# A gated linear attention followed by top-1 experts: heads kept on their own partitions, rows turned on VectorE, experts taken in order of their counts

## The chip, the cores and the metric

One Trainium2 chip, one core of it. The metric is the device time of one execution in microseconds (us), as the median of several runs. A profiled execution gives the trace from which the durations here are read.

## What is computed

The reference has two blocks. The first is a recurrence with a complex gate per head and feature. The state is a 48 x 48 matrix per head, and 4 batches of 8 heads run over 768 steps:

```python
for t in range(S):
    new_re = ar * S_re - ai * S_im          # ar, ai: the gate, its magnitude cut at 0.999
    new_im = ar * S_im + ai * S_re
    S_re, S_im = new_re + kv, new_im        # kv = outer product of k[t] and v[t]
    y[:, :, t] = einsum('bhd,bhde->bhe', q[:, :, t], S_re)
```

The second takes the 3072 rows of 384 numbers (8 heads side by side) and sends each to the one of 8 experts with the largest logit:

```python
logits = x @ w_gate; expert_idx = argmax(logits, axis=1); gate_w = softmax(logits)[expert_idx]
out[mask] = gate_w[mask, None] * (maximum(x[mask] @ w1[e], 0.0) @ w2[e])   # w1: 384 x 1024, w2: 1024 x 384
```

With the reference's inputs the experts 0 to 7 get 354, 406, 392, 388, 370, 421, 338 and 403 rows. All numbers are float32.

## The kernel before

**Attention.** The recurrence is turned into products over chunks of 128 steps. A gate's logarithm and angle are summed along time, and with them q and k are scaled by a cosine and by a sine factor; the scaled q and k of a head are then one operand of 96 rows (48 features of part 0, the cosine, and 48 of part 1, the sine). A chunk's rows of y are the masked products of its own q and k with v, plus q times the state left by the chunks before.

The *front* (function `front`) makes the scaled q and k in ten units of 128, 256 or 384 steps, with the features of 8 heads on 128 partitions in three groups: heads 0 to 2 on partitions 0 to 47, heads 3 to 5 on 48 to 95, heads 6 and 7 on what is left. ScalarE takes logarithms, exponentials, arctangents and sines, VectorE (and GpSimd for two multiplications per unit, from unit 3 on: `EARLY`) the rest. The last two operations of a unit on VectorE are the products with the cosine (into `hz`, part 0) and with the sine (into `Z`, part 1). Then nine transfers per unit on the SP queue (L334) move rows within SBUF, so that in `hz` every head has its part 0 on partitions 0 to 47 and its part 1 on 48 to 95.

A *chunk* (function `chunk`) is done on TensorE, for all 8 heads at once:
- *turned keys* (L361): eight turnings of a head's k into `kt`, in two groups of four; not in the last chunk of a batch;
- *scores* (L368): eight products k by q, 96 rows deep, four into each of two banks of PSUM; VectorE masks each bank (`am`);
- *old state* (L380): eight products of the state `sb` with q, from the second chunk of a batch on. The outputs have 48 partitions, of even heads at 0, of odd heads at 64, so neighbours lie on two column halves of the array;
- *values* (L387): eight products of v with `am`, in two groups of four (heads 0 to 3, 4 to 7), added to the same bank as the old state. Even and odd heads alternate in each group;
- *new state* (L395): eight products of the turned keys with v, into bank 5, copied to `sb`; not in the last chunk;
- *turning products* (L403): four, which bring y into rows of tokens and make the logits beside them.

A `route` after some chunks (the last three after chunks 3, 5 and 6 of the last batch) finds each row's expert and place on VectorE, and GpSimd sends the rows with gate and token number to `xs_hbm` (L464), where each expert has 448 places.

The order of all these operations on all engines is the list `ORDER`, in base 36; a class `Plan` with costs and dependences lies behind it. Every engine runs its part of the list strictly in order, and a DMA issue on SP waits in its place too.

**Experts.** After the last route some checks set a flag (`again`) for a slow general version behind a branch, which these inputs don't take. For each expert in turn, SP loads both weights (1536 KB each, three buffers each) and its 448 rows (L575, L578). TensorE turns the rows in twelve pieces (L586), which ScalarE and VectorE copy to `xrt`. The *first layer* (L597) is 8 x 3 products of 448 columns, cut at zero into `ht` by ScalarE (L603) and VectorE (L600). The *second layer* (L611) is 3 x 8 products of 384 columns for the first 384 rows. The 64 rows left over of two neighbouring experts share one group (L626), 64 columns of the array each. VectorE scales the outputs (L566), and GpSimd scatters them (L555). The order comes from `Plan.order`, a list scheduler on costs and dependences.

Of the kernel before, what the change touches and what calls it, by code (L numbers as in the profile page):

```python
# [22 lines left out]
G = 3  # L23

BLOCKS = ((0, 48, 0, 3, 0, 0), (48, 96, 0, 3, 3, 0), (96, 128, 0, 2, 6, 0), (96, 112, 2, 3, 6, 32), (112, 128, 2, 3, 7, 32))
TU = 384
NB = 3
EARLY = 3
# [6 lines left out]
MINC = 256  # L35
# [12 lines left out]
0 2 1l 3 4 5 1n 3n 1o 1p 6 7 8 1q 1r 9 1s a b d 3p 1t 3q c 1u f 1 e 14 3r g 1v 1w j 3o 1m 24 3s 1y 1x  # L48
l m 3t k h 4r n o p 27 i q r s 3u 26 1z 20 t u 25 21 28 3v 23 22 29 v 10 3w 2a 46 6n z 2b 11 15 2c 3x 3y
17 2d 40 y 2e 12 w 7r 2f 6p 3z 6q 6r 16 13 x 18 2g 99 42 2j 41 48 43 19 47 49 44 1d 1a 2i 6s 6t 2k 6u 2l 2m 4b 2n 45  # L50
6v 4a 9b 1b 2r 2o 4c 1c 2h 9c 2s 6w 9d 1e 6x 6y 4d 4e 2v 6o 4f 4g 76 4i 4j 1f 4h 78 9e 1i 9s 6z 2t cb 1g 38 2p 70 2w 9f
4m 9g 72 71 9h 2u 1h 3c 77 3a 79 75 2x 4n 73 2q 7a 39 2z 2y 74 4l 7b 9i cd 30 31 7c ce 3d 4u 9j 4q 32 7d 4k 4p 7e 36 3e
1k cf 3g 9u 3b 4o 37 4v 7f 3f 1j 9t 3h 4y 5b 9a 7g 4w 3i 7h 3j 4s 4t 33 4x 4z 35 5c cg 50 54 9m 51 7i 5f ch 34 55 ci 59
9k 7k 9l 7l 52 5a 53 3k 5g 7j 5q 9n 5d eu cj 5s 9o 5e 3m 7q 5h 9v 7p 7n 5r 7o ck 5l 5j 9r 3l 5t 9w 7z 56 ew 5i 7m cl co
9p 9q 9x 5m 80 cc ex cn 7x 7v 5k 81 9y 82 58 5u 5w cu 9z cm 5v 57 8h 7w 8f 5x 5n a0 5o 7y cw 86 ev a1 5p 8b ey 5y cq 8i
ad cv a2 df a4 8d cp a6 a3 87 8g 8c 8e 8y 83 ez cx a7 84 8w a5 85 5z 60 f0 8n ct f1 8j 8z 8s cy 88 aa 61 8l 62 8o 8u 8x
8t 8k a9 cr 68 94 ab f2 8m ac 90 a8 hu ak 69 89 8v 6a cs 91 f3 ag cz ai 8a d0 f4 fd 8p al hv ae 92 f7 d1 b1 d2 d3 ah f6
95 af 8r ax 6b av d4 93 aj 8q hw am az d5 d6 an hx f5 ay ao aq fg d7 d9 fe db f8 96 ap bc b2 da 98 aw ar 6e f9 97 6c 63
fa de 64 d8 b3 bd b4 kw b5 hy 65 b0 hz dd 6d as be i0 fc 66 i1 ff b6 dc au fb dg fh b7 b8 67 di bf 6h 6k dh i2 fi dm 6j
# [77 lines left out]
def gateloop_then_moe(ctx, tc, gates, qk, gates_u, qk_u, v, wg, w1, w2, out):  # L137
# [11 lines left out]
    def tt(o, a, b, op, eng=None):  # L149
        (eng or nc.vector).tensor_tensor(out=o, in0=a, in1=b, op=op)  # L150
# [47 lines left out]
    with ExitStack() as att:  # L198
# [25 lines left out]
        def dve2(n):  # L224
            return n * 0.00104 + 0.06
# [18 lines left out]
        def front(u):  # L244
# [66 lines left out]
            for part in (0, 1):  # L311
                for p0, p1, g0, g1, h0, d0 in BLOCKS:
                    if part == 0 and p0 == 0:
                        continue
# [481 lines left out]
```

## Time and profile before

| | us |
|---|---|
| median of 3 runs | 570.27 |
| lowest, highest | 564.31, 571.41 |
| the profiled execution | 565.04 |
| its span, first to last instruction | 563.2 |

The profile is of one execution. A page gives busy times and the span in 40 slices. Answers of the trace give busy times by stretch, groups by line, waits, and the order of time, in which neighbouring instructions of one line are merged into one row. A float32 product shows as two records on TensorE (PE), a turning as one. [...]

### The profile page before, as it was taken

Reading aid. Unit: us, or ns where it says so; the run is one execution under the profiler, and the core shown is the slowest. Engines: PE = TensorE matmul, PEld = TensorE weight load, DVE = VectorE, ACT = ScalarE, POOL = GpSimd, SP = SyncE. Lnnn points to the kernel's source line nnn. Section 1 sums busy time; section 2 is a strip of 40 time slices with the busy share of each in tenths; the row PEclk is TensorE's granted clock in tenths of the full one; section 3 lists DMA queues with packets and bytes.
Section 4 is the critical chain, followed back from the end, with each engine's and each line's share of the span. In section 5 each row is a group of like instructions: output and inputs, shape, how many; then the busy total and the mean of one; then the engine's idle time right before and its main releaser. Section 6 shows DMA issues by size and latency. Waiting matters only on the chain. (4 is left out here: it accounts for less than half of the span.)

```text
span 563.2 us, 7082 instructions
## 1 busy us (share of the span) xinstructions
PE 485.5 (86%) x2785; PEld 329.1 (58%) x2785; DVE 240.8 (43%) x412; ACT 214.0 (38%) x313; POOL 94.3 (17%) x106
## 2 busy tenths in 40 slices
PE   0045998798898799729999999999999999999995
PEld 0034997787798699614555555555555555555552
DVE  3999989989798684401111021110111011211011
ACT  6999898979788565201100011000011000111000
POOL 3012214206240533200001020020100010200022
PEclk9999999989799799959999999999999999999998
DMA  8486959578399865199502272214443021400010
GB/s 320 131 252 163 256 149 336 116 214 216 118 208 217 245 113 180 44 318 387 205 14 82 111 263 64 98 42 169 160 143 120 14 69 57 145 2 14 1 38 34
DMA packets 25384, 82.03 MB, mean 146 GB/s; under 512 B 3600, under 2 KB 16816, under 8 KB 20896
## 3 DMA queue, kind: packets, MB, share of 16 engines
q1 hardware_dynamic: 22016, 72.04, 42.8%
q0 software_dynamic: 3328, 9.47, 4.6%
q8 instruction: 24, 0.39, 0.3%
q14 instruction: 16, 0.13, 0.1%
HBM read 54.32 MB, written 12.62 MB: 119 GB/s over the span
## 5 line engine op out<-in xcount | busy, mean ns | idle before, releaser
L597 PE MATMUL bank<-xrt,w1b 128*128 128x448 f32 x384 | 149.4, 544 | 2.1 <-ACT xrt L588 2.1
L611 PE MATMUL bank<-w2b,ht 128*128 128x384 f32 x384 | 128.4, 488 | 0.0
L597 PEld LDWEIGHTS bank<-xrt,w1b 128*128 128x128 f32 x384 | 73.0, 192 | 70.5 <-issue 64.8
L611 PEld LDWEIGHTS bank<-w2b,ht 128*128 128x128 f32 x384 | 72.1, 190 | 51.9 <-issue 6.9
L603 ACT ACTIVATE ht<-bank 128x448 f32<-128x448 f32 x32 | 17.4, 544 | 174.0 <-PE bank L597 174.0
L555 POOL DMA_INDIRECT out_dram<-yo,xr x24 | 23.5, 978 | 292.2 <-DVE yo L566 288.1
L368 PE MATMUL bank<-hz 96*128 96x128 f32 x384 | 61.6, 315 | 7.7 <-DMA hz<-Z 6.5
L600 DVE TENSOR_SCALAR ht<-bank 128x448 f32<-128x448 f32 x32 | 20.0, 625 | 111.4 <-PE bank L597 111.4
L368 PEld LDWEIGHTS bank<-hz 96*128 96x128 f32 x384 | 54.8, 221 | 12.0 <-issue 6.1
L361 PE MATMUL bank<-ident,hz 96*128 96x96 f32 x160 | 23.6, 279 | 38.0 <-DMA hz<-Z 35.4
L566 DVE TENSOR_SCALAR yo<-bank,xr 128x384 f32<-128x384 f32 x24 | 14.8, 618 | 79.4 <-PE bank L611 79.4
L588 ACT COPY xrt<-bank 128x384 f32<-128x384 f32 x16 | 7.6, 478 | 94.0 <-PE bank L586 93.9
L361 PEld LDWEIGHTS bank<-ident,hz 96*128 96x128 f32 x160 | 18.7, 161 | 40.6 <-issue 38.1
L236 ACT ACTIVATE AB<-AB 128x1152 f32<-128x1152 f32 (+2 forms) x40 | 38.3, 968 | 7.1 <-DMA AB<-in_gates_u_dram 5.2
L150 DVE TENSOR_TENSOR am<-bank,causal 128x512 f32<-128x512 f32 x48 | 32.3, 680 | 14.5 <-PE bank L368 14.5
L150 DVE TENSOR_TENSOR Z<-Z,AB 128x1152 f32<-128x1152 f32 (+4 forms) x20 | 34.1, 1704 | 1.2 <-DMA hz<-Z 0.3
L403 PE MATMUL bank<-turn,yt 128*128 128x104 f32 x192 | 28.0, 292 | 6.7 <-ACT yt L391 3.9
L464 POOL DMA_INDIRECT xs_hbm<-xg,slot x24 | 26.1, 1088 | 40.1 <-DVE cumb L461 14.8
L150 POOL TENSOR_TENSOR AB<-AB,C 128x1152 f32<-128x1152 f32 (+2 forms) x7 | 18.0, 2567 | 87.3 <-ACT C L236 77.2
L387 PE MATMUL bank<-am,v 128*48 128x128 f32 x384 | 30.5, 299 | 2.2 <-DVE am L150 2.2
L395 PE MATMUL bank<-v,kt 128*96 128x48 f32 x320 | 31.6, 253 | 0.0
L395 PEld LDWEIGHTS bank<-v,kt 128*96 128x96 f32 x320 | 30.1, 171 | 1.8 <-issue 1.5
(110 smaller groups left out, 499.3 us busy)
## 6 DMA issues: line engine op xcount, KB each, us to landing
w1b<-in_w_dram SPq DMA_DIRECT2D x8, 1536.0 KB, 14.0
w2b<-in_w_dram SPq DMA_DIRECT2D x8, 1536.0 KB, 7.0
AB<-in_gates_u_dram SPq DMA_DIRECT2D x6, 1152.0 KB, 7.1
Z<-in_qk_u_dram SPq DMA_DIRECT2D x6, 1152.0 KB, 8.2
hz<-Z SPq DMA_DIRECT2D x12, 432.0 KB, 8.7
xr<-xs_hbm SPq DMA_DIRECT2D x8, 579.0 KB, 7.8
v<-in_v_dram SPq DMA_DIRECT2D x8, 576.0 KB
hz<-hz SPq DMA_DIRECT2D x6, 432.0 KB, 5.5
```

What stands on the lines that cost most here:

```text
L150: (eng or nc.vector).tensor_tensor(out=o, in0=a, in1=b, op=op)
L236: lambda: nc.scalar.activation(o, i, func=f, scale=scale, bias=bias, **kw), r, w, tag)
L361: nc.tensor.transpose(KT[hf][:, (h % 4) * 96:(h % 4) * 96 + 96], hk[:, h], ident[0:96, 0:96])
L368: nc.tensor.matmul(SC[hf][:, (h % 4) * 128:(h % 4) * 128 + 128], lhsT=hk[:, h], rhs=hq[:, h], start=True, stop=True)
L387: nc.tensor.matmul(YT[ps, (h // 2) * 128:(h // 2) * 128 + 128], lhsT=V[:, cl, h * D:h * D + D], rhs=am[2 * par + hf][:, h % 4, :], start=( ...
L395: nc.tensor.matmul(ST[0:96, h * D:h * D + D], lhsT=kt[par][:, h * 96:h * 96 + 96], rhs=V[:, cl, h * D:h * D + D], start=(c == 0 and h == 0 ...
L403: nc.tensor.matmul(XT[:, p * 104:p * 104 + 104], lhsT=yt[par][:, p * 128:p * 128 + 128], rhs=turn[:, p, :], start=True, stop=True)
L464: i = nc.gpsimd.indirect_dma_start(out=xs_hbm[:, :], out_offset=bass.IndirectOffsetOnAxis(ap=R[slot][:, c:c + 1], axis=0), in_=xg[:, (g0 + ...
L555: i = nc.gpsimd.indirect_dma_start(out=out[:, :], out_offset=bass.IndirectOffsetOnAxis(ap=index, axis=0), in_=y, in_offset=None, bounds_ch ...
L597: nc.tensor.matmul(HB[hb][:, 0:CAP], lhsT=w1b[ws][:, c:c + 128], rhs=xrt[s][:, d, :], start=(d == 0), stop=(d == DT - 1))
L600: M.add("DVE", 0.6, lambda f_=f_, hb=hb: nc.vector.tensor_scalar_max(ht[s][:, f_, :], HB[hb][:, 0:CAP], 0.0), (("H", hb),), (("ht", s, f_),))
L611: nc.tensor.matmul(OB[ob][:, 0:DM], lhsT=ht[s][:, f_, j * 128:j * 128 + 128], rhs=w2b[ws][:, f_ * DM:f_ * DM + DM], start=(f_ == 0), stop= ...
```

## The change

**Heads stay where they were made.** The features of heads 0 to 5 lie in pairs: in group g head 2g on partitions 0 to 47, head 2g+1 on 64 to 111. Heads 6 and 7 fill partitions 48 to 63 and 112 to 127, 16 features in each group. Part 0 stays in a new tile `cz`, part 1 in `Z` (four buffers); only heads 6 and 7 are moved, into `cm`, in four transfers per unit. For heads 0 to 5 each product over 96 rows becomes two over 48 rows which are added in PSUM: first part 0, then part 1. Turning goes through a matrix `order` that puts the 96 used columns first. The two groups of value products are now the even and the odd heads.

```diff
+            def f():
+                for g in range(G):
+                    for part in range(2):
+                        for h in (2 * g, 2 * g + 1):
+                            nc.tensor.matmul(SC[h % 2][:, g * 128:g * 128 + 128], lhsT=wide[part][side(h), g, 1], rhs=wide[part][side(h), g, 0],
+                                             start=(part == 0), stop=(part == 1), skip_group_check=True)
+            P.add("PE", 1.45, f, ZK[0] + ZK[1], (("SC", 0), ("SC", 1)))
+
+            def f():
+                for j in range(2):
+                    nc.tensor.matmul(SC[j][:, 384:512], lhsT=last2[:, j, 1], rhs=last2[:, j, 0], start=True, stop=True)
+            P.add("PE", 0.50, f, MK, (("SC", 0), ("SC", 1)))
...
-                P.add("PE", 0.97, f, (("sb", 1 - par),) + hkey(range(H)), tuple(YK))
+                    for g in range(G):
+                        for part in range(2):
+                            for h in (2 * g, 2 * g + 1):
+                                s0 = part * G * D + g * D
+                                nc.tensor.matmul(YT[side(h), g * 128:g * 128 + 128], lhsT=sb[1 - par][side(h), s0:s0 + D],
+                                                 rhs=wide[part][side(h), g, 0], start=(g == 0 and part == 0), stop=False, skip_group_check=True)
+                P.add("PE", 1.43, f, (("sb", 1 - par),) + ZK[0] + ZK[1], (("YT", 0), ("YT", 1)))
...
             for hf in range(2):
                 def f(hf=hf):
-                    for h in range(4 * hf, 4 * hf + 4):
-                        ps = slice(64 * (h % 2), 64 * (h % 2) + D)
-                        nc.tensor.matmul(YT[ps, (h // 2) * 128:(h // 2) * 128 + 128], lhsT=V[:, cl, h * D:h * D + D],
-                                         rhs=am[2 * par + hf][:, h % 4, :], start=(c == 0 and h < 2), stop=True,
-                                         skip_group_check=True)
+                    for g in range(4):
+                        h = 2 * g + hf
+                        nc.tensor.matmul(YT[side(h), g * 128:g * 128 + 128], lhsT=V[:, cl, h * D:h * D + D],
+                                         rhs=am[2 * par + hf][:, g, :], start=(c == 0 and g == 0), stop=True, skip_group_check=True)
```

(`side(h)` is partitions 0 to 47 for even and 64 to 111 for odd heads.) In TensorE's order, the rows around two groups of old state (`sb`) and of values (`am`) in a chunk of the second batch, before:

```order
L380 MATMUL bank_65<-hz_150,sb_147 48x128 x8
L387 MATMUL bank_65<-am_139,v_137 48x128 x4
L368 MATMUL bank_62<-hz_150 128x128 x4
L395 MATMUL bank_66<-v_137,kt_142 96x48 x8
L387 MATMUL bank_65<-am_138,v_137 48x128 x4
L403 MATMUL bank_67<-turn,yt_145 128x104 x4
L380 MATMUL bank_65<-hz_150,sb_146 48x128 x8
```

And in the changed kernel, in a chunk of the first batch (`cz` is part 0, `Z` part 1, `cm` the two moved heads; L395 and L401 old state, L408 values, L365 and L367 turned keys, L429 turning products):

```order
L395 MATMUL bank_65<-cz_158,sb_173 48x128 x2
L395 MATMUL bank_65<-Z_151,sb_173 48x128 x2
L395 MATMUL bank_65<-cz_158,sb_173 48x128 x2
L395 MATMUL bank_65<-Z_151,sb_173 48x128 x2
L395 MATMUL bank_65<-cz_158,sb_173 48x128 x2
L395 MATMUL bank_65<-Z_151,sb_173 48x128 x2
L365 MATMUL bank_63<-order,cz_158 128x128 x3
L401 MATMUL bank_65<-cm_159,sb_173 48x128 x2
L429 MATMUL bank_67<-turn,yt_171 128x104 x4
L365 MATMUL bank_64<-order,Z_151 128x128 x3
L408 MATMUL bank_65<-am_168,v_163 48x128 x4
L367 MATMUL bank_63<-ident,cm_159 128x96
```

Eight products of old state have become twelve and two, part by part, and a group of four values now has one mask tile (`am_168`: the odd heads) and so one column half.

Smaller edits here: the first multiplication of a unit is always on VectorE, the sixth on GpSimd from unit 1 on (`ON_POOL = "6"`, `EARLY = 1`), and each such GpSimd operation waits for the VectorE operation listed before it. The list `ORDER` is new (it begins `0 2 3 4 1i 5 6 7 3l 1k` in place of `0 2 1l 3 4 5 1n 3n 1o 1p`). The weights of expert 0 (`wA1`, `wA2`) are loaded during the attention.

**Rows turned on VectorE, experts by count.** The rows of an expert come in four transfers, each into 32 partitions, so that 32 x 32 blocks turned on VectorE give `xrt` directly; TensorE turns nothing.

```diff
+            for q in range(4):
+                M.add("SP", 0.65, lambda q=q: nc.sync.dma_start(
+                    xr[s][32 * q:32 * q + 32, 0:nb, :], row(r, 0, 32 * nb).rearrange("(b p) w -> p b w", p=32)[:, :, 32 * q:32 * q + XW]),
...
+            for d in range(DT):
+                M.add("DVE", 0.00105 * nt + 0.06, lambda d=d: nc.vector.transpose(
+                    xrt[s][:, d, 0:nt].rearrange("p (b i) -> p b i", i=32), xr[s][:, 0:nb, d * 128:d * 128 + 32]),
```

Expert 0 comes first; the others follow in falling order of their counts. The ranking is made on VectorE behind the last route (`perm`), and SP reads each rank's expert into a register (`values_load`), from which the addresses of rows and weights follow. The ranks have fixed rooms, so the first layer has fewer columns, and the rows left over beyond 384 share two groups: two ranks with 64, four with 32.

```diff
+ROOM = (448, 448, 416, 416, 416, 416, 384, 384)
+LEFT = ((0, 0, 64, 0, 0), (1, 0, 64, 0, 64), (2, 0, 32, 1, 0), (3, 0, 32, 1, 32), (4, 0, 32, 1, 64), (5, 0, 32, 1, 96))
```

The second layer's weights have five buffers and the first layer's two (beside expert 0's own); gate and token number come in transfers of their own (`hg`, `hs`). TensorE's order before, where the first two experts meet (L586 turns rows):

```order
L597 MATMUL bank_63<-xrt_1983,w1b_1975 128x448 x3
L586 MATMUL bank_61<-ident,xr_1982 128x128 x3
L586 MATMUL bank_62<-ident,xr_1982 128x128 x3
L597 MATMUL bank_64<-xrt_1983,w1b_1975 128x448 x3
L586 MATMUL bank_61<-ident,xr_1982 128x128 x3
L586 MATMUL bank_62<-ident,xr_1982 128x64 x3
L611 MATMUL bank_66<-w2b_1978,ht_1985 128x384 x4
L597 MATMUL bank_65<-xrt_1984,w1b_1976 128x448 x3
```

The turnings are gone from there, and VectorE now has them, for the second expert before its last cut of the first (L683 is the cut at zero):

```order
L667 STREAM_TRANSPOSE xrt_2364<-xr_2362 128x448 x3
L683 TENSOR_SCALAR ht_2366<-bank_62 128x384
L683 TENSOR_SCALAR hl_2368<-bank_62 128x64
L683 TENSOR_SCALAR ht_2366<-bank_64 128x384
L683 TENSOR_SCALAR hl_2368<-bank_64 128x64
L683 TENSOR_SCALAR ht_2366<-bank_62 128x384
L683 TENSOR_SCALAR hl_2368<-bank_62 128x64
L667 STREAM_TRANSPOSE xrt_2365<-xr_2363 128x448 x3
L683 TENSOR_SCALAR ht_2366<-bank_64 128x384
```

On TensorE all eight first-layer groups of the second expert follow those of the first directly, and the third expert's first layer stands behind six groups of four second-layer products. On SP the order behind the first rows is: the second expert's first weights and rows, then the second weights of the second, the first and second weights of the third, the second weights of the fourth and fifth, and only then the third expert's rows.

## Rows read from the trace of the kernel before

**Rows 1.** The page: busy us (share) xinstructions, and VectorE in 40 slices.

```profile
PE 485.5 (86%) x2785; PEld 329.1 (58%) x2785; DVE 240.8 (43%) x412; ACT 214.0 (38%) x313; POOL 94.3 (17%) x106
...
DVE  3999989989798684401111021110111011211011
```

**Rows 2.** Busy us by stretch: PE, PEld, DVE, ACT, POOL, then PEclk, DMA share, GB/s.

```profile
70.00:200.00 130.00, 117.21 (x1217) 106.67 (x1216) 111.94 (x157) 107.09 (x154) 39.25 (x25) 0.93 0.75 198
200.00:235.00 35.00, 34.26 (x412) 31.93 (x411) 19.68 (x64) 18.78 (x37) 12.24 (x15) 1.00 0.49 124
245.00:255.00 10.00, 4.99 (x15) 3.21 (x16) 1.08 (x3) 0.96 (x2) 0.00 (x0) 0.50 1.05 371
255.00:275.00 20.00, 20.00 (x62) 10.47 (x61) 3.74 (x8) 3.02 (x6) 0.00 (x0) 0.98 0.82 313
```

**Rows 3.** The longest wait on moved rows; VectorE's second product of unit 0.

```profile
PE bank L361 <- DMA hz<-Z: 35.4, 3, 33.5
...
24.75 0.96 DVE L150 TENSOR_TENSOR Z<-Z,AB 128x768 f32<-128x768 f32 x1
```

**Rows 4.** TensorE in order of time, attention: start us, us, engine, line, what.

```profile
75.00 1.48 PE L395 MATMUL bank<-v,kt 128*96 128x48 f32 x16
76.31 0.51 PE L361 MATMUL bank<-ident,hz 96*128 96x96 f32 x4
76.67 1.06 PE L403 MATMUL bank<-turn,yt 128*128 128x104 f32 x8
...
201.73 0.65 PE L387 MATMUL bank<-am,v 128*48 128x128 f32 x8
202.30 1.56 PE L395 MATMUL bank<-v,kt 128*96 128x48 f32 x16
...
207.65 1.08 PE L380 MATMUL bank<-hz,sb 96*48 96x128 f32 x16
208.56 1.04 PE L387 MATMUL bank<-am,v 128*48 128x128 f32 x16
209.54 1.16 PE L368 MATMUL bank<-hz 96*128 96x128 f32 x8
210.53 1.04 PE L403 MATMUL bank<-turn,yt 128*128 128x104 f32 x8
```

**Rows 5.** TensorE's L586 alone, behind the hole.

```profile
252.90:558.00 305.10, 11.47 (x84) 9.61 (x84) 1.00 0.29 103
```

**Rows 6.** TensorE in order of time, experts.

```profile
281.10 7.90 PE L611 MATMUL bank<-w2b,ht 128*128 128x384 f32 x24
...
288.84 6.93 PE L597 MATMUL bank<-xrt,w1b 128*128 128x448 f32 x18
...
295.60 5.32 PE L611 MATMUL bank<-w2b,ht 128*128 128x384 f32 x16
...
317.94 5.38 PE L626 MATMUL bank<-w2b,ht 128*64 128x384 f32 x32
...
323.25 2.20 PE L611 MATMUL bank<-w2b,ht 128*128 128x384 f32 x6
```

**Rows 7.** The hole between the stages, in order of time.

```profile
234.48 1.14 PE L403 MATMUL bank<-turn,yt 128*128 128x104 f32 x8 [0.74 <-ACT yt L391]
...
241.67 0.38 SPq L575 DMA_DIRECT2D xr<-xs_hbm  x1
...
249.52 2.89 PE L586 MATMUL bank<-ident,xr 128*128 128x128 f32 x12 [9.77 <-DMA xr<-xs_hbm]
...
252.90 9.62 PE L597 MATMUL bank<-xrt,w1b 128*128 128x448 f32 x21 [0.50 <-ACT xrt L588]
```

**Rows 8.** VectorE's last front product, one multiplication; the moves of L334.

```profile
213.76 0.96 DVE L150 TENSOR_TENSOR Z<-Z,AB 128x768 f32<-128x768 f32 x1
...
L150 DVE TENSOR_TENSOR AB<-AB,C 128x1152 f32<-128x1152 f32 x1 | 1.4, 1359 | 0.4 <-ACT C L236 0.4
...
DMA to landing us min/median/max: 2.3/5.0/10.0
```

More of the change, by code (lines that the diff above doesn't have):

```diff
@@ L189, in gateloop_then_moe @@
     ones_b = const([128, 128], "ones_b", 1.0, BF16)
+    num_i = const([128, E], "num_i", dt=I32)
+    nc.gpsimd.iota(num_i, pattern=[[1, E]], base=0, channel_multiplier=0)
+    num = const([128, E], "num")
+    nc.vector.tensor_copy(num, num_i)
+    room = const([128, E], "room")
+    for r in range(E):
+        nc.gpsimd.memset(room[:, r:r + 1], float(ROOM[r]))
+    wA1, wA2 = const([128, DT * F], "wA1"), const([128, FT * DM], "wA2")
     cum = const([128, E], "cum")
@@ new lines, in chunk, with side @@
+            zi, ci, mi = u % NZ, u % NC, u % 2
+            wide = [y[:, 0:2 * G * T].rearrange("p (g x t) -> p g x t", g=G, x=2)[:, :, :, o:o + 128] for y in (cz[ci], bZ[zi])]
+            last2 = cm[mi][:, 0:4 * T].rearrange("p (j x t) -> p j x t", j=2, x=2)[:, :, :, o:o + 128]
+            ZK = [(("cz", ci),), (("Q", zi), ("K", zi))]
+            MK = tuple(("cm", mi, part, j) for part in range(2) for j in range(2))
+            def side(h):
+                return slice(64 * (h % 2), 64 * (h % 2) + D)
@@ L399, in chunk @@
-                P.add("ACT", act_t(384) - 0.06, lambda: nc.scalar.copy(sb[par], ST[0:96, 0:DM]), ("ST",), (("sb", par),))
+                    for g in range(G):
+                        for part in range(2):
+                            for h in (2 * g, 2 * g + 1):
+                                s0 = part * G * D + g * D
+                                nc.tensor.matmul(ST[side(h), s0:s0 + D], lhsT=kt[par][:, part, g * 96 + D * (h % 2):g * 96 + D * (h % 2) + D], rhs=V[:, cl, h * D:h * D + D],
+                                                 start=(c == 0 and g == 0 and part == 0), stop=True, skip_group_check=True)
@@ L504, in gateloop_then_moe @@
                     nc.scalar.preload_act_table_set("natural_log_exp_and_others" if P.cur == "LE" else "trig_and_small")
-                o["fn"]()
+                ins = o["fn"]()
+                if o["port"] and o["eng"] == "DVE":
+                    behind = ins
+                elif o["port"] and behind is not None:
+                    tc.add_manual_dep(ins.ins, behind.ins.name, mybir.DependencyInfo(mybir.DependencyClass.Sync, mybir.DependencyReason.DATA),
+                                      reason="both engines share a port of SBUF")
@@ L637, in gateloop_then_moe @@
+        with tc.manual_schedule():
+            M.add("SP", 0.0, lambda: None, (), ("perm",))
+            loads(0)
+            for r in range(E):
+                if r + 1 < E:
+                    loads(r + 1)
+                expert(r)
+                for sh in range(2):
+                    if max(x[0] for x in LEFT if x[3] == sh) == r:
+                        shared(sh)
+                if r < E - 1:
                     M.add("POOL", 1.0, lambda: nc.gpsimd.drain(), ("scattered",), ("drained",))
-                if e == 2:
+                if r == 2:
```

423 lines of the change are left out of this document (222 added, 201 removed).

## Prediction

> **What bounds the kernel now.** I read the page first (its busy times and slices), then busy time by stretch, the longest waits, and the order of time of TensorE in both halves. There are two stages. Up to about 236 us the attention runs with three engines nearly full; from 253 us the experts run and TensorE is full to the end: it is 485.5 us busy in all, while VectorE falls to one or two tenths in the second half [rows 1]. [...]
>
> In the attention stage no single engine is the bound all the way. From 70 to 200 us TensorE shows 117 of 130 us busy, VectorE 112, ScalarE 107; but TensorE finished 1217 records there, 9.4 per us, and 412 in the 35 us behind, 11.8 per us [rows 2]. At that later rate the 1217 would have taken 103 us, so TensorE has about 27 us of room before 200 us, some of it lost to a granted clock of 0.93. Behind 200 us TensorE alone is full; the last product of part 1 on VectorE (213.76 us) ends 21 us before the last turning product does [rows 7, 8]. So extra work on TensorE first fills that room and then moves the end.
>
> **The attention: work on TensorE.** Each term is for one chunk at the later, full rate, by the time from the start of one group to the start of the next. All 24 chunks have scores and values; the groups on keys, new state and old state exist in 20 of them.
> Value products: eight lie on alternating column halves and take 0.98 us together, or 0.57 us for four where the two groups stand apart [rows 4]; 1.07 for eight is the mean of both. In the new order each group of four has all its outputs on one half. No row of before shows that. The bounds: nothing added, if they still overlap; or the price of four full-width products one after the other, 0.99 us [rows 4], so 1.98. I take the latter, since the four share one half: +0.91 x 24 = +21.8.
> Old-state products: 8 on alternating column halves take 0.91 us [rows 4], 0.114 each. The new 14 in pairs cost 1.59: +0.68 x 20 = +13.6. Twelve of them one by one, 12 x 0.25 + 0.23 = 3.2: +46.
> Score products: 2 x 0.99 before. Now 12 on two row halves and 2 full. In pairs 12 x 0.114 + 2 x 0.25 = 1.87: -0.11 x 24 = -3. One by one 14 x 0.25 = 3.5: +36.
> No row of before shows two products side by side on row halves; the nearest, the column halves, do run side by side (0.91 for eight against 0.99 for four of full width), so I take pairs for both and keep the other ends for a rival.
> Turned keys: four of 96 columns take 0.36, so eight 0.72; eight mostly of 128 columns, at the 11.47 us for 84 of [rows 5], take 1.09: +0.37 x 20 = +7 (nothing at the least).
> New state: 8 take 1.31 us. The new 14 load as many weight columns in all (768), so the same; fully in pairs 0.7, by the shortest spacing of a record (0.91/16) 1.6. I take 1.2, nearer the first: -2.
> Changes between full, half and quarter layout: 0.98 against 0.91 us for eight products, where the next group has another layout [rows 4], 0.07 each, some three more per chunk: +5.
> Sum +42 us. The 27 us of room take most, and about 4 belong to chunks before 70 us, where TensorE starves anyway. 11 are left.
>
> Less is to be gained from the transfers. The first product waited until 33.5 us for moved rows, the largest of 35.4 us of such waits, though VectorE had made them by 25.7 [rows 3]. Six of eight heads now need no move, so TensorE can start up to 7.8 us sooner. I count 1 of them, since the fronts behind still arrive one by one. Net: the attention ends **10 us later**, at about 246 us.
>
> VectorE: one product per unit from unit 3 on comes over from GpSimd (1.36 us for a full unit [rows 8], 6 full-unit equivalents, +8), one leaves for units 1 and 2 (1.7 equivalents, -2.3). With 18 us idle of 130 [rows 2] that is covered, unless the front becomes the bound: then the last front product still ends near 215 us, and one move (5.0 us median [rows 8]) and a chunk's groups follow, some 8 us by the sum of the terms above. 228 us is the floor. GpSimd's product now waits for the VectorE operation listed before it; behind it on GpSimd stand the next unit's product and the sending of rows, and GpSimd, 39 us busy of 130 [rows 2], has the time: 0. SP issues 4 moves per unit in place of 9, plus two 1.5 MB loads; its queue is shorter.
>
> **The hole.** Now: last turning product done at 235.6, rows asked for at 241.67, landed by 249.5, first expert product at 252.90: 17.3 us [rows 7]. The first two steps stay. The weights of expert 0 are already there, but its rows come as four pieces of 32 partitions by 14 blocks of 1152 bytes, 2.06 MB instead of 0.69. At 371 GB/s [rows 2] they take 5.6 us, at the 264 GB/s that the attention's transfers reach per full share (198/0.75 [rows 2]) 7.8; to this the 2.3 us of the shortest landing [rows 8], 6.05 us before it, and three turns on VectorE. A turn of 448 elements is not in the trace; 1152 elements take 1.36 us on VectorE [rows 8], hence 0.53 each, 1.6 in all (double at worst, half at best). Together 14.7 to 19.4; I take 16.8, with a transfer rate between the two rows: -0.5.
> [...] No row here shows such a piece.
>
> **The experts.** TensorE is full, so what leaves it leaves the time.
> First layer: 18 records of 448 columns take 6.76 us [rows 6], so 1.677 ns per column and product. Rooms of 448, 448, 4 x 416, 2 x 384 are 256 columns less than 8 x 448; times 24 products: 6144 x 1.677 = -10.3.
> Turning on TensorE: 84 records, 11.47 us behind the hole [rows 5], go to VectorE, which is busy 3.7 us of 20 there [rows 2]: -11.5.
> Left-over rows: four groups of 5.31 us [rows 6] become two. Two halves of 64 columns overlap now; whether four of 32 do isn't shown: -10.6, or -5.3 if not. I take -10.6, since the halves overlap in full.
> The second layer and the tail behind the last product stay. The turns (1.6 us per expert) and the cuts at zero in two pieces lie beside 30 us of TensorE's work per expert. Sum **-32.4 us**.
> New waits: SP reads an expert's number before each load; behind it stand all later loads. The third expert's rows stand behind six weight loads of 1.57 MB and the second's rows of 2.06, with their own 1.92 that is 13.4 MB. At 313 GB/s [rows 2] they land 58 us after the attention's end (the first expert's rows having landed at 15), at 264 GB/s after 66 us; TensorE wants them 17 us after that end, plus two first layers of 18.0 and six groups of four second-layer products of 2.58 [rows 6], less 1.6 for the turn: 67. Covered, barely. If late, VectorE stands at that turn and the scaling of outputs behind it waits too.
>
> **Sum.** +10 - 0.5 - 32.4 = -22.9 on the profiled execution's 565.04 us (563.2 of span and 1.84 around it): **542 us**. The median of before is 570.27, 0.9% above that execution; the 2% lines, about what a measurement of this kernel can tell from no change, lie at 559 and 582.
>
> **Rivals.**
> A, the forecast: 542, own range 527 to 557. Chance 0.57.
> B, old-state products don't pair: here both row halves write the same bank of PSUM, while the scores write two. They cost 3.2 us instead of 1.59, and TensorE's room is used up: 1.6 x 20 = +32, 574 us, no change. For it: no row of before has two row halves in one bank; against: the column halves, also in one bank, overlap. 0.11. [...]
> C, the other side: row halves never overlap. Scores +39 (3.5 for 1.87) and old state +32 on the forecast: the attention ends near 317 us, 613 in all, slower. It decides from an attention end of 280 us (32.9 gained behind it, 11 for 2%). Against it: the planner's new figures, 1.45 and 1.43 us for such twelve, and its old ones (0.96 for four scores, 0.97 for the old state) agree with 0.99 and 0.91 [rows 4]. 0.11.
> D, the value groups overlap after all, or the front sets the end: 228 us, 18 sooner than A: 524. 0.13.
> E, the threefold row bytes starve the experts: at 200 GB/s the third expert's rows land at 82 instead of 67: +15, 557. For it: 371 GB/s were seen with long weight rows only. 0.08.
> That the experts don't follow the new order, the program taking its fallback, would be seen as a time many times longer; the counts (338 to 421) fit the rooms. I give it nothing.
>
> **Numbers.** Faster by over 2%: A but for its upper end (0.56), D and most of E, 0.74. Same: B and the rest, 0.15. Slower: C, 0.11. The range takes A, D, E and B, 520 to 576.
>
> **What would show it.** In the profile after: the value group of four at 0.95 us or more (A) or near 0.57 (D); twelve old-state and twelve score products each within 1.6 us (A), or about 3 (B, C); the last turning product at 240 to 252 us; no turning group on TensorE in the experts; shared groups of 5.3 us, two in number; no wait of TensorE on a turn of VectorE beyond the first expert. An attention end before 232 or after 262 us would make my sum wrong in the first stage, an expert stage outside 268 to 280 us in the second.

## The result, and the profile after

| | before | after |
|---|---|---|
| median, us | 567.29 (4 runs, 560.00 to 571.41) | 542.28 (4 runs, 541.94 to 543.05) |
| profiled execution | 565.04 | 542.31 |
| end of the last turning product of the attention | 235.6 | 244.6 |
| from there to the first expert product | 17.3 | 19.8 |
| from there to the end of the last expert product | 304.2 | 271.05 |

The changed kernel takes 0.9648 of the time of before, with a 95% interval of 0.9583 to 0.9714: faster. (This ratio leaves out the two executions of before at 570.27 and 571.41 us, which fell in a slower state; the medians of the table alone would give 0.956.) The three stages give +9.0, +2.5 and -33.2, together -21.7; the tail behind the last product is 0.9 shorter, so the span falls by 22.6.

Busy times by stretch in the kernel after, in the columns of [rows 2] (PEclk is the clock granted to TensorE, as a share of its full speed):

```profile
70.00:200.00 130.00, 128.85 (x1667) 111.84 (x1666) 111.83 (x161) 110.14 (x153) 29.26 (x22) 1.00 0.56 168
200.00:235.00 35.00, 34.74 (x461) 30.91 (x463) 20.79 (x54) 18.54 (x31) 12.30 (x12) 1.00 0.26 70
245.00:255.00 10.00, 0.55 (x5) 0.21 (x4) 4.96 (x36) 0.69 (x2) 0.99 (x1) 0.63 0.37 89
255.00:275.00 20.00, 10.65 (x24) 5.32 (x25) 3.08 (x7) 0.60 (x2) 0.00 (x0) 0.67 1.07 238
```

Beside [rows 2], TensorE is now full from 70 to 200 us as well (128.85 of 130 in place of 117.21), and the clock granted there is 1.00 in place of 0.93. In the hole the transfer engines are at a full share, 1.07, but move 238 GB/s; [rows 2] had 371 at 1.05.

TensorE in order of time in the kernel after (start, us, engine, line, what), some ten us of a full stretch; L408 is a value group, L376 and L382 scores, L395 and L401 old state, L418 and L422 new state, L429 turning products:

```profile
190.27 1.04 PE L408 MATMUL bank<-am,v 128*48 128x128 f32 x8
191.24 1.14 PE L429 MATMUL bank<-turn,yt 128*128 128x104 f32 x8
...
200.99 1.55 PE L408 MATMUL bank<-am,v 128*48 128x128 f32 x16
202.48 0.49 PE L376 MATMUL bank<-cz 48*128 48x128 f32 x4
202.80 0.39 PE L376 MATMUL bank<-Z 48*128 48x128 f32 x4
...
204.01 0.71 PE L382 MATMUL bank<-cm 96*128 96x128 f32 x4
204.56 0.49 PE L365 MATMUL bank<-order,Z 128*128 128x128 f32 x3
204.89 1.04 PE L429 MATMUL bank<-turn,yt 128*128 128x104 f32 x8
205.86 0.42 PE L395 MATMUL bank<-cz,sb 48*48 48x128 f32 x4
...
207.30 0.43 PE L401 MATMUL bank<-cm,sb 96*48 96x128 f32 x4
207.56 0.71 PE L418 MATMUL bank<-v,kt 128*48 128x48 f32 x24
208.20 0.54 PE L422 MATMUL bank<-v,kt 128*96 128x48 f32 x4
208.57 0.27 PE L367 MATMUL bank<-ident,cm 96*128 96x96 f32 x1
```

By the starts: a value group alone takes 0.97 us (190.27 to 191.24; elsewhere up to 1.01), two that are neighbours, as in ten chunks of the 24, take 1.49; twelve scores 1.53 and the two full ones 0.55; twelve old-state products 1.44 and the two full ones 0.26; the new state 1.01.

The hole in the kernel after, in order of time; L647 asks for row pieces, L651 for weights, L667 is VectorE's turn and L678 the first layer:

```profile
243.46 1.14 PE L429 MATMUL bank<-turn,yt 128*128 128x104 f32 x8 [0.73 <-ACT yt L411]
...
250.79 2.19 SPq L647 DMA_DIRECT2D xr<-xs_hbm  x4
...
253.78 0.38 SPq L651 DMA_DIRECT2D w1b<-in_w_dram  x1
254.43 10.24 SPq L647 DMA_DIRECT2D xr<-xs_hbm  x4
263.65 1.70 DVE L667 STREAM_TRANSPOSE xrt<-xr 128x448 f32<-128x448 f32 x3 [12.27 <-DMA xr<-xs_hbm]
...
264.35 5.88 PE L678 MATMUL bank<-xrt,wA 128*128 128x448 f32 x10 [13.15 <-DVE xrt L667]
```

The rows are asked for 6.2 us behind the attention's end, as before (6.05 in [rows 7]); they land 12.9 us later. From TensorE's experts in the kernel after, the shared group of four pieces of 32 and the last second layers:

```profile
447.28 5.37 PE L707 MATMUL bank<-w2b,hl 128*32 128x384 f32 x64
...
519.76 15.64 PE L694 MATMUL bank<-w2b,ht 128*128 128x384 f32 x48
```

Of the list of waits of that kernel, this is the only one of TensorE on a turn (us in all, times, longest), the one in the hole:

```profile
PE bank L678 <- DVE xrt L667: 13.2, 1, 13.2
```

VectorE turns the third expert's rows 64.7 us behind the attention's end, having stood 6.0 us for them:

```profile
309.27 1.60 DVE L667 STREAM_TRANSPOSE xrt<-xr 128x416 f32<-128x416 f32 x3 [5.98 <-DMA xr<-xs_hbm]
```

### The profile page after: what moved, and what is told of

Its sections match the earlier page's. It is cut to its first block, busy times and chain, and to the rows that moved or that the text cites. A ratio compares the mean times of both kernels' runs of the same rounds, so it can differ in the third digit from the quotient of the medians.

```text
span 540.6 us, 8473 instructions
## 1 busy us (share of the span) xinstructions
PE 474.9 (88%) x3425; PEld 326.9 (60%) x3425; DVE 246.6 (46%) x450; ACT 213.8 (40%) x325; POOL 83.0 (15%) x112
## 5 line engine op out<-in xcount | busy, mean ns | idle before, releaser
L678 PE MATMUL bank<-xrt,w1b 128*128 128x416 f32 (+2 forms) x336 | 118.3, 509 | 0.0
L694 PE MATMUL bank<-w2b,ht 128*128 128x384 f32 x336 | 110.8, 487 | 0.0
L678 PEld LDWEIGHTS bank<-xrt,w1b 128*128 128x128 f32 x336 | 63.9, 190 | 52.0 <-issue 37.5
L611 POOL DMA_INDIRECT out_dram<-yo,hg x24 | 23.6, 982 | 262.4 <-DVE yo L622 172.2
L683 DVE TENSOR_SCALAR ht<-bank 128x384 f32<-128x384 f32 x32 | 17.6, 556 | 90.5 <-PE bank L678 90.5
L376 PE MATMUL bank<-cz 48*128 48x128 f32 x288 | 31.4, 295 | 26.8 <-DVE cz L158 26.8
L408 PE MATMUL bank<-am,v 128*48 128x128 f32 x384 | 46.2, 279 | 0.6 <-DVE am L158 0.6
L158 POOL TENSOR_TENSOR Z<-Z,C 128x1152 f32<-128x1152 f32 (+2 forms) x9 | 20.5, 2273 | 153.6 <-ACT C L258 81.0
L376 PEld LDWEIGHTS bank<-cz 48*128 48x128 f32 x288 | 22.6, 193 | 29.9 <-DVE cz L158 26.8
L408 PEld LDWEIGHTS bank<-am,v 128*48 128x48 f32 x384 | 37.2, 124 | 4.4 <-DVE am L158 1.1
L158 DVE TENSOR_TENSOR Z<-Z,AB 128x1152 f32<-128x1152 f32 (+4 forms) x20 | 33.2, 1660 | 0.8 <-ACT AB L258 0.4
L678 PE MATMUL bank<-xrt,wA 128*128 128x448 f32 x48 | 20.2, 584 | 13.2 <-DVE xrt L667 13.2
L376 PE MATMUL bank<-Z 48*128 48x128 f32 x288 | 29.0, 279 | 0.7 <-DVE Z L158 0.7
L429 PE MATMUL bank<-turn,yt 128*128 128x104 f32 x192 | 26.5, 281 | 0.7 <-ACT yt L411 0.7
L667 DVE STREAM_TRANSPOSE xrt<-xr 128x416 f32<-128x416 f32 (+2 forms) x24 | 13.5, 593 | 26.2 <-DMA xr<-xs_hbm 18.7
```

The source lines that it names most:

```text
L158: return (eng or nc.vector).tensor_tensor(out=o, in0=a, in1=b, op=op)
L376: nc.tensor.matmul(SC[h % 2][:, g * 128:g * 128 + 128], lhsT=wide[part][side(h), g, 1], rhs=wide[part][side(h), g, 0], start=(part == 0), ...
L408: nc.tensor.matmul(YT[side(h), g * 128:g * 128 + 128], lhsT=V[:, cl, h * D:h * D + D], rhs=am[2 * par + hf][:, g, :], start=(c == 0 and g ...
L429: nc.tensor.matmul(XT[:, p * 104:p * 104 + 104], lhsT=yt[par][:, p * 128:p * 128 + 128], rhs=turn[:, p, :], start=True, stop=True)
L611: i = nc.gpsimd.indirect_dma_start(out=out[:, :], out_offset=bass.IndirectOffsetOnAxis(ap=index, axis=0), in_=y, in_offset=None, bounds_ch ...
L678: nc.tensor.matmul(HB[hb][:, 0:nt], lhsT=a[:, c:c + 128], rhs=xrt[s][:, d, 0:nt], start=(d == 0), stop=(d == DT - 1))
```

## The experiments

Each kernel is the one after with the edit shown, unless the text says otherwise. "Attention's end" is the end of the last turning product; in the four runs below that leave the attention untouched it stands at 245.8 to 246.0 us, against 244.6 in the profile above; the clock granted from 200 to 235 us is 0.95 in these four and 1.00 there.

**Value groups with both column halves.**

```diff
-                    for g in range(4):
-                        h = 2 * g + hf
+                    for h in range(4 * hf, 4 * hf + 4):
+                        g = h // 2
...
-                                         rhs=am[2 * par + hf][:, g, :], ...
+                                         rhs=am[2 * par + h % 2][:, g, :], ...
```

In the list the two groups of a chunk are put next to each other, at the place of the later one.

> The two value groups of a chunk take heads 0 to 3 and 4 to 7, as in the kernel before, so column halves alternate, and stand next to each other. Theory 1 (TensorE is full from 70 us to the end of the attention, and a value group on one half is serial): eight products take 1.0 to 1.15 us from start to start, where two groups apart now take 2.0 and two neighbours 1.49; 19 chunks x 0.9 + 5 x 0.4 = 19 us less work, cut off by the floor of 228 us that the fronts set. The attention ends at 228 to 232 us, in all about 529. Rival (the fronts already hold the attention's end): it ends at 240 or later, in all 538 or more, and TensorE shows the missing work as waits. Rival (a group costs the same on two halves): no change, 542.

530.59 us (0.9391 of before, 0.9305 to 0.9476). TensorE in order of time:

```profile
205.29 1.05 PE L408 MATMUL bank<-am,v 128*48 128x128 f32 x16
206.17 0.71 PE L418 MATMUL bank<-v,kt 128*48 128x48 f32 x24
...
230.89 1.14 PE L429 MATMUL bank<-turn,yt 128*128 128x104 f32 x8 [0.73 <-ACT yt L411]
```

Eight products now take 0.88 us (205.29 to 206.17), and the attention ends at 232.0, 12.6 us sooner than in the kernel after. Theory 1 holds: the grouping by halves, not the fronts, cost the attention those 12.6 us. Two things are in the edit, though, groups with both halves and their place next to each other, and no run has one without the other. In the kernel after the two groups were neighbours in ten chunks, not in five as expected, so about 22 us of work were taken out (14 x 1.12 + 10 x 0.61), and more than a third of that didn't reach the end.

**Row halves not alternating.**

```diff
-                for g in range(G):
-                    for part in range(2):
-                        for h in (2 * g, 2 * g + 1):
+                for h in (0, 2, 4, 1, 3, 5):
+                    g = h // 2
+                    for part in range(2):
```

The same edit in the old state.

> In the scores and the old state the six even and odd heads no longer alternate: first the three even heads (partitions 0 to 47), then the three odd ones (64 to 111). The same products, another order. Theory 1 (two products lie side by side because neighbours stand on different row halves of the array): twelve products take about 3.0 us (12 x 0.25) instead of 1.54 and 1.45; 24 x 1.46 + 20 x 1.55 = +66 us on a TensorE that is full, of which up to 8 lie in idle time before 70 us: the attention ends at 300 to 310, in all about 603. Rival (products of 48 rows are simply shorter, or any two neighbours overlap): within 5 us of 542.

585.78 us; the attention ends at 288.4. Twelve old-state products in order of time:

```profile
250.92 0.42 PE L395 MATMUL bank<-cz,sb 48*48 48x128 f32 x2
251.18 0.38 PE L395 MATMUL bank<-Z,sb 48*48 48x128 f32 x2
...
251.83 0.42 PE L395 MATMUL bank<-cz,sb 48*48 48x128 f32 x4
...
253.28 0.42 PE L401 MATMUL bank<-cm,sb 96*48 96x128 f32 x4
```

They take 2.36 us in place of 1.44 (and twelve scores 2.53 in place of 1.53): 0.22 us for one alone. Only where the order passes from even to odd heads (251.83) do two stand side by side. (2.36 - 1.44) x 20 + (2.53 - 1.53) x 24 = 42.4, and the attention's end moved by 43.8 (some of it by the clock: 0.97 was granted from 70 to 200 us, 1.00 in the kernel after). So the side-by-side work on row halves is what makes the change possible, in two banks (scores) and in one (old state) alike; my price of 0.25 for one alone was too high.

**What delays the first expert's rows.** Three runs. In the first, the load of the second expert's first weights, and with it all of SP's later loads, waits for the first expert's turns, which are listed right behind its pieces:

```diff
+                    if r == 1:
+                        tc.add_manual_dep(i.ins, turned[2].ins.name, ...)
```

> All loads behind the first expert's four row pieces (the second's first weights at once behind them) wait on SP until the first expert's rows have been turned. Theory a (the pieces share the transfer engines with the weights and rows behind them): at 250 GB/s alone they land 2.3 + 8.2 = 10.5 us after the first issue instead of 12.9, the first expert product starts 2 to 3 us sooner (5 sooner at 371 GB/s), and if the later loads still come in time the whole is 539 to 540. Theory b (pieces of 1152 bytes on 32 partitions are themselves that slow, 160 GB/s): they land as before, the product starts at the same distance from the attention's end (19.8 us), and the whole is 542 or more. In both, a wait of TensorE on the second expert's rows or weights near 20 us behind the first expert product would be the price of holding.

543.57 us (0.9637 of before, 0.9556 to 0.9718). Busy times by stretch, and the hole in order of time:

```profile
255.00:257.00 2.00, 0.00 (x0) 0.00 (x0) 0.00 (x0) 0.00 (x0) 0.00 (x0) 0.50 1.10 194
257.00:259.00 2.00, 0.00 (x0) 0.00 (x0) 0.00 (x0) 0.00 (x0) 0.00 (x0) 0.50 1.07 199
259.00:261.00 2.00, 0.00 (x0) 0.00 (x0) 0.00 (x0) 0.00 (x0) 0.00 (x0) 0.50 1.10 197
```

```profile
251.98 1.90 SPq L647 DMA_DIRECT2D xr<-xs_hbm  x4
...
264.42 1.70 DVE L672 STREAM_TRANSPOSE xrt<-xr 128x448 f32<-128x448 f32 x3 [11.89 <-DMA xr<-xs_hbm]
```

Alone on the transfer engines the pieces still need 12.4 us (12.9 with company): theory b. The engines are full and move 194 to 199 GB/s.

In the second run each piece is narrower:

```diff
-XW = 288
+XW = 160
...
-                    ... xr[s][:, 0:nb, d * 128:d * 128 + 32]),
+                    ... xr[s][:, 0:nb, d % 2 * 128:d % 2 * 128 + 32]),
```

> Each row piece is cut from 288 to 160 numbers (1152 to 640 bytes), so the last third of every row is left out of the experts (the third turn takes the first third again). As many pieces, 0.56 of the bytes. Theory a (the landing goes by bytes): (12.4 - 2.3) x 0.56 = 5.6 us behind the shortest landing, the first expert product stands 15.4 us behind the attention's end instead of 19.8, and the whole is 537 to 538. Theory b (it goes by the number of pieces): still 19.8 within half a microsecond, 542.

539.03 us. The rows in order of time:

```profile
252.16 1.90 SPq L647 DMA_DIRECT2D xr<-xs_hbm  x4
...
260.32 1.70 DVE L667 STREAM_TRANSPOSE xrt<-xr 128x448 f32<-128x448 f32 x3 [7.57 <-DMA xr<-xs_hbm]
```

8.2 us: less the shortest landing of 2.3 [rows 8], 5.9 in place of 10.1 (12.4 - 2.3, the pieces alone), a ratio of 0.58 where the bytes have 0.56. So the landing goes by bytes, not by the number of pieces.

In the third the last two pieces of the first expert are issued by ScalarE:

```diff
+                M.add("ACT" if r == 0 and q > 1 else "SP", 0.65, lambda q=q: (nc.scalar if r == 0 and q > 1 else nc.sync).dma_start(
```

> Of the first expert's four row pieces the last two are issued on ScalarE's queue, beside the first two on SP's. The same pieces and bytes. Theory a (while one transfer writes 32 partitions only those 32 take data, and pieces on one queue follow each other): two pieces at a time, so 2.3 + 5 us to landing instead of 12.4 to 12.9, the first expert product about 15 us behind the attention's end instead of 19.8, the whole 537 to 538. Theory b (the rows come at some 200 GB/s from where they lie, whatever partitions they go to): hole 19 to 20, the whole 541 to 542.

544.75 us. Busy times by stretch:

```profile
255.00:257.00 2.00, 0.00 (x0) 0.00 (x0) 0.00 (x0) 0.00 (x0) 0.00 (x0) 0.50 1.09 331
257.00:259.00 2.00, 0.00 (x0) 0.00 (x0) 0.00 (x0) 0.00 (x0) 0.00 (x0) 0.50 1.08 316
259.00:261.00 2.00, 0.00 (x0) 0.00 (x0) 0.00 (x0) 0.00 (x0) 0.00 (x0) 0.50 1.20 371
```

The expectation had two outcomes, and neither came: the engines moved 316 to 371 GB/s instead of 195, but the rows were turned only at 265.06, 12.9 us behind their first issue. The trace's list of transfers shows how. Up to 259 us nothing but row pieces was under way, so on two queues they did move at 331 and 316 GB/s from 255 to 259 us, as theory a has it; 1732 of their 1792 runs of 1152 bytes had started by 260 us, 7.9 us behind the first issue. The last 60, all of ScalarE's queue, straggled in up to 263.7, beside the weights, which SP's queue had begun to load at 259. So the pieces came faster until the weights moved beside them, and in the end no sooner. What was measured is 194 to 199 GB/s for pieces on one queue, in the run that holds the rest back, and 331 and 316 for pieces on two queues that fill both halves of the partitions. Two queues into the same half weren't tried, so whether the halves or the second queue made the difference isn't shown; nor were two queues with the weights held back, so what they would save isn't measured.

**The first expert turned on TensorE.** On top of the mixed value groups; its rows come as in the kernel before, 0.69 MB on 128 partitions, and are turned by twelve products with four copies.

> With mixed value groups; and the first expert's rows alone are loaded as in the kernel before (128 partitions, 0.69 MB) and turned by twelve products on TensorE and four copies. Theory a (the row pieces are what made the hole longer): the hole is that of before, 17.3 us instead of 19.9, so 2.5 us less than 530.6, about 528. Rival (the loads behind set the landing): hole near 19.5, 530 or more, since twelve turning products are added.

528.52 us (0.9296 of before, 0.9185 to 0.9407). The hole in order of time:

```profile
234.88 1.14 PE L429 MATMUL bank<-turn,yt 128*128 128x104 f32 x8 [0.73 <-ACT yt L411]
...
242.40 0.38 SPq L654 DMA_DIRECT2D xr<-xs_hbm  x1
...
246.47 2.69 PE L682 MATMUL bank<-ident,xr 128*128 128x128 f32 x12 [3.85 <-DMA xr<-xs_hbm]
```

The rows land 4.1 us behind their issue in place of 12.4, and the first layer starts at 249.71, 13.7 us behind the attention's end in place of 19.9: better than the 17.3 of before, where weight loads had been issued just ahead of the rows and just behind them (that these made the difference isn't shown). Of these 6.2 us the median shows 2.1, for the attention ended 4 us later in this execution, without an edit to it. The last experiments ask why.

**Fillers in the hole and before 50 us.** All three runs build on the kernel with mixed groups and the first expert turned on TensorE. The first adds twelve products of 512 columns without use in the hole:

```diff
+            for k in range(12):
+                nc.tensor.matmul(HB[3][:, 0:512], lhsT=wA1[:, 0:128], rhs=wA1[:, 0:512], start=True, stop=True)
```

> As the kernel with the first expert turned on TensorE, and twelve products without use (512 columns, into a free bank) behind the attention's last checks, so that TensorE works in the hole. Theory (the half clock at the start of the experts, which is granted for about 3.5 us of work there, comes from the idle hole): turning and first layer start at full clock, 1.3 + 1.6 us sooner than without, about 525. Rival (the level rises at a time of its own, or falls again before the rows land): as without them, 528, or later by what the twelve overrun.

528.01 us (0.9350, 0.9270 to 0.9429). The granted clock stays at 1.00 from 235 us on, where the kernel without fillers shows 0.66 from 235 to 255; the first layer starts 12.5 us behind the attention's end in place of 13.7, and the experts take 269.15 us in place of 270.65. That is 2.7 us, where 2.9 were expected; the medians don't show them, since the attention's end, at 236.5, is again late (two of the fillers were put ahead of its last products). This is the first chunks' work in the kernel with mixed groups alone, and then in the one with the first expert turned on TensorE, with the same code up to there:

```profile
52.23 0.39 PE L376 MATMUL bank<-Z 48*128 48x128 f32 x4
52.45 0.39 PE L376 MATMUL bank<-cz 48*128 48x128 f32 x4
```

```profile
53.55 0.64 PE L376 MATMUL bank<-Z 48*128 48x128 f32 x4
53.98 0.64 PE L376 MATMUL bank<-cz 48*128 48x128 f32 x4
```

The same four records stand 0.22 us apart in one and 0.43 in the other, half the rate. The row of the clock shows 1.00 in both, but it says nothing here: the trace's first record of a granted clock starts at 49.4 us in the first and at 68.4 in the second, and a row counts time without a record as full. In both that first record grants 1.00, and from its start on the groups stand at the full rate; up to there they stand at half of it. The first record of the kernel before starts at 68.2 us, as its old-state groups show in order of time, and that of the kernel after at 49.7:

```profile
64.48 1.95 PE L380 MATMUL bank<-hz,sb 96*48 96x128 f32 x16
...
70.89 1.08 PE L380 MATMUL bank<-hz,sb 96*48 96x128 f32 x16
```

The second run adds products without use (128 columns) between 36 and 50 us as well:

```diff
+                    for _ in range({6: 18, 8: 5, 13: 8}.get(npe, 0)):
+                        nc.tensor.matmul(bank[7][:, 384:512], lhsT=ident, rhs=ident, start=True, stop=True)
```

> As the kernel with mixed value groups, the first expert turned on TensorE and twelve products without use in the hole; and 31 products of 128 columns without use in the gaps of TensorE between 36 and 50 us. Theory (that TensorE's groups take twice as long up to 51 us in some executions and up to 68 in others comes from its idle gaps before 50 us): full rate from 44 us at the latest, in every execution; the attention ends at 231 to 233, the whole 522 to 525 with a spread of runs under 2 us. Rival (the rate rises when it will): 525 to 531, spread as before.

525.62 us (0.9274, 0.9213 to 0.9334), runs from 523.55 to 526.11: the fastest median of all, though slower than expected, with a spread of 2.6 us in place of 2. The first clock record now starts at 37.9 us; but the fillers themselves waited 2.8 us for VectorE, which still used their bank, and the granted clock fell to 0.50 from 44.7 to 51.5 us. From there on all groups stand at full rate; the attention ends at 234.2. In the hole, with the same twelve fillers as before, the granted clock fell as well, from 246.1 to 252.9 us, and the experts take 272.1 us in place of 269.15. The last run puts them into a bank that nobody reads and sets 16 of 512 columns into the hole, behind the attention's last products:

> Mixed value groups, the first expert turned on TensorE, 34 products without use between 36 and 50 us (into a bank that nothing reads by then, so that they wait for nothing), and 16 in the hole, placed so that none comes ahead of the attention's last products. Theory (TensorE's rate before 70 us and at the start of the experts goes by its idle time): full rate from 44 us on, no half-rate stretch at the experts' start, the attention ends at 231 to 233, the first layer starts 12.5 us later, the experts take 269; 520 to 522, the runs within 2 us. Rival (the fillers cost in the chain of moves and masks before 50 us what the rate gives): the attention ends at 234 or later, 524 and more.

528.61 us (0.9342, 0.9292 to 0.9393). The first half came as expected but for the spread: full rate from 39.7 us, the attention's end at 232.1, six runs within 2.9 us. The same 24 records in the kernel with mixed groups alone, and then here:

```profile
45.74 1.20 PE L418 MATMUL bank<-v,kt 128*48 128x48 f32 x24
```

```profile
46.05 0.74 PE L418 MATMUL bank<-v,kt 128*48 128x48 f32 x24
```

The second half was mis-sized:

```profile
235.27 16.87 PE L566 MATMUL bank<-wA 128*128 128x512 f32 x32 [0.26 <-DVE cnt L564]
...
252.19 1.53 PE L688 MATMUL bank<-ident,xr 128*128 128x128 f32 x12
```

I had counted a product of 512 columns at 0.44 us, which is one record; it has two, and up to 241.1 us the granted clock was 0.50. The fillers overran the rows by some 9 us (rows asked for at 239.35, as long a landing as above ends at 243.4) and gave back all that was won.

**How near is the fronts' floor, and what VectorE's extra product costs.** The first run leaves out, with mixed value groups, part 1 of the scores of heads 0 to 5:

```diff
-                    for part in range(2):
+                    for part in range(1):
```

> With mixed value groups, and the scores made from part 0 alone: six of twelve products of 48 rows in each chunk are left out (the sine's share of the scores). 24 x 0.75 = 18 us less on TensorE. Theory (TensorE is still full with mixed groups, and the fronts set a floor of 228 us, as forecast): the attention ends at 226 to 230 instead of 232.0, about 527 in all. Rival (no floor near): it ends at 214 to 216, about 513. Rival (the floor is reached already): 231 to 233, 530.

531.52 us; the attention ends at 233.7. In this stretch TensorE waits and VectorE is the fullest engine, if only by 1.5 us:

```profile
70.00:200.00 130.00, 120.71 (x1581) 101.72 (x1581) 122.16 (x187) 116.62 (x164) 35.46 (x26) 0.96 0.57 172
```

So of some 18 us less on TensorE nothing reaches the end in this execution. But it ran at half rate up to 67 us, which may hide up to 4 us, by the pair of executions above. Without these the end would stand near 230, as the first theory has it. So a floor is near the 232.0 of the mixed groups; whether it lies there or at 228 this one run doesn't decide. The second gives the product that came to VectorE back to GpSimd, by `ON_POOL = "16"`.

> The product that the change took from GpSimd goes back to it, in all units but the first; nothing else. VectorE has 8832 columns less, some 10 us. Theory (TensorE is the bound of the attention, VectorE's products are covered, as forecast): the attention ends within 2 us of 244.6, the whole 540 to 544. Rival (VectorE's front is what TensorE waits for): 3 to 8 us sooner. Rival (a product on GpSimd takes longer and its unit arrives later): 2 to 5 us later.

545.36 us; the attention ends at 247.8, 1.9 us later than in the four runs named above, though VectorE is 108.5 us busy in place of 111.8 from 70 to 200 us. By its bounds that is the last rival, 3.2 us behind the 244.6. So the moved product cost nothing, as forecast. That it won 2 us isn't shown by one execution, in which TensorE's full rate also came late (first clock record at 52.6 us; 49.9 to 51.2 in the four).

**The order of counts undone**, with rooms of 448 for all and four shared groups of two halves:

```diff
-ROOM = (448, 448, 416, 416, 416, 416, 384, 384)
-LEFT = ((0, 0, 64, 0, 0), (1, 0, 64, 0, 64), (2, 0, 32, 1, 0), ...)
+ROOM = (448,) * 8
+LEFT = tuple((r, 0, 64, r // 2, 64 * (r % 2)) for r in range(8))
```

> The order of counts is undone in its effect: every expert has a room of 448 and 64 rows left over, in four shared groups of two halves; rows are still turned on VectorE. Theory 1 (TensorE is full in the experts, so each product removed there was time): first layer +256 columns x 24 x 1.677 ns = +10.3, two more groups of 5.3 = +10.6, in all 563, the expert stage 292 us. Rival (part of the gain of the smaller rooms is lost in waits, or the gain came from the turns alone): less than +14.

565.50 us. The first expert product starts at 265.19, and the last rows of TensorE are

```profile
552.43 5.43 PE L694 MATMUL bank<-w2b,ht 128*128 128x384 f32 x16
```

so the stage takes 292.7 us, 21.6 more than after; 20.9 were worked out. The other 11.6 of the 33.2 us are then what turning on TensorE had cost, 11.5 by [rows 5].

## Why the prediction held, point by point

- **The time.** 542 forecast, 542.28 measured, in the case named as likeliest (A). Of the stages, the attention's end moved by 1.0 us less than forecast on the profiled execution, the hole came out 3.0 us worse, and the experts and the tail behind them 1.7 better. So the sum is nearer than its terms.
- **Pairs on row halves** (rivals B and C). Twelve products within 1.6 us was the sign of A; they take 1.53 and 1.44. The run with the halves apart shows that this rests on the alternation, and would have cost 43.8 us. The one bank that B feared cost nothing in the old state here: both row halves write it, to different partitions, side by side (1.44 us for twelve, 2.36 with the halves apart).
- **Value groups** (rival D). 0.97 to 1.01 us for a group alone, where 0.99 was taken. Unforeseen: where the two groups of a chunk are neighbours they take 1.49, the end of one beside the start of the other (10 chunks of 24).
- **The sum of the attention.** By the starts above, against the prices of [rows 4]: values +17 (14 x 0.90 + 10 x 0.42), old state +15.8, scores +2.4, turned keys +8 (1.14 a chunk, the mean behind 70 us, in place of 0.72), new state -6 (1.01 in place of 1.31), changes of layout within these: +37 in place of +42. The end moved by 9.0 (10 in the four other runs). So two errors cancelled, which is luck: the sum was 5 too high, and of the 27 us of room only some 23 (37 - 4 - 1 - 9) took work. The 9.0 has some luck in it too: TensorE stood at half its rate up to 68.2 us in the execution of before and up to 49.7 in that of after. With mixed groups such a difference made 4 us of the end; what it made in the kernel before, which had more room, no run shows.
- **The front floor.** Whether "228 us" was low isn't decided: the end came no sooner than 232.0, with 18 us less on TensorE at 233.7 in an execution with a late rise of the rate. The working behind it was wrong: VectorE's last front product ends at 232.4 in the kernel after, not near 215; VectorE's order holds masks, which wait for scores, ahead of it, so it moves with TensorE.
- **The hole.** The step that failed is the price of the pieces, "a transfer rate between the two rows" of 264 and 371 GB/s. It is 195: (12.9 - 2.3) us in place of some 7. The upper end of 19.4 fell 0.4 short. The two rates were read from transfers of other shapes, so the price was an estimate, and the hole became 2.5 us longer in place of 0.5 shorter. The turns themselves were right (1.7 us for 1.6), but the first product stands only 0.7 us behind their start, so 0.9 us came back.
- **The experts.** -33.2 for -32.4. The two shared groups take 5.3 us each, four pieces of 32 as two of 64; no turn other than the first is waited for, so the third expert's rows were in time (rival E): landed 64.7 us behind the attention's end, inside the 58 to 66 worked out, though the first expert's pieces came at E's 200 GB/s. SP's reading of numbers cost TensorE nothing.

## What to carry to other kernels

Products that fill a part of the array were worth splitting here because neighbours in the order stand on different halves (twelve old-state products took 1.44 us so, and 2.36 with the halves apart); put that into the order by hand, down to every group, for groups in which all stand on one half cost 12.6 us here. A transfer that costs nothing beside work must be priced by its own shape where it is alone on the path: rows on 32 partitions, on one queue, came at 194 to 199 GB/s in place of the 371 of [rows 2] and with three times the bytes, and turning one expert in the old way shortened the hole by 6 us.

## What the runs showed that I had not expected

In these executions TensorE works at half its rate in the first 50 to 70 us (0.43 us for the scores that take 0.22 later), with gaps of up to 6.2 us in the kernel after between its groups, and the row of the granted clock hides it: the trace has no clock record there, which a row shows as 1.00, and the first record starts where the rate rises. That time differs between executions of the same code (49.4 or 68.4 us) and shifts the attention's end by 4 us. In the twelve profiled executions without fillers in those gaps it lies between 49.4 and 68.6 us, in the two with them at 37.9 and 39.7. So the fillers bring the rise forward; they don't hold the rate, for in one of the two the granted clock fell again from 44.7 to 51.5 us, TensorE having waited from 43.7 to 46.5.

In the hole of the kernel after, the granted clock falls from 1.00 to 0.50 in the slice from 247 to 248 us, TensorE having been idle but for three small products since 244.6, and is 1.00 again from 269, TensorE having worked since 264.35. With twelve fillers in the hole it stayed at 1.00 in one profiled execution, in which TensorE's last wait ahead of the rows was 1.5 us, and fell at 246.1 us in the other, in which it was 1.7.
